# Two decode attentions on one core: the last group of heads ends in column form, with a new load order at the end

## The chip, the cores and the metric

The kernel runs on one core of a Trainium2 chip. The metric is device time in microseconds (us), the median of several executions. "Span" is the time from the first to the last instruction in the profile of one execution; it is 1.6 to 2.0 us less than the device time, except in three executions (2.9 to 3.4 us). Engines are called PE (matrix multiply), DVE (vector), ACT (scalar) and SP (here it only issues DMAs); POOL (general purpose) has no part in the ending. PE's granted clock, the share of full speed that PE was allowed, is recorded with each profile: in the records of the kernel before it is 1.00 or 0.50 and nothing else (another value in a table below is the mean of a stretch). A PE at full clock is called warm, one at half clock cold. "A's last p.v" is the last product of exponentials and V for problem A. All outputs are right.

Where a ratio of two kernels is given, it is the mean time of one kernel's runs over that of the other's in the same rounds, with a 95% interval. It is therefore not quite the ratio of the medians quoted beside it.

## The reference, cut to what matters

Problem A is decode attention of one token over 32 heads with 16384 keys each; problem B is the same over the last 4096 keys of its own cache. The head size is 128, and all data are bf16.

```python
q = (x @ wq) ...                       # one token, 32 heads of 128
scores = einsum("bhqd,bhkd->bhqk", q, k) * (128 ** -0.5)
p = softmax(scores)
o = einsum("bhqk,bhkd->bhqd", p, v)
out = o.reshape(1, 1, 32 * 128) @ wo   # 512 columns for A, 512 for B
```

K and V are read once: 336 MB of the 352 MB moved. The rest is weights.

## The kernel before

Work goes in units: four single heads of A (4 MB of K, 4 MB of V each), then one unit of B with four heads (also 4 + 4 MB), eight times over. A unit has two chunks of 64 keys per partition. For each chunk, DVE multiplies K by q (`prod`) and adds halves (`half`), PE sums further (`red`), DVE finishes the scores (`sc`), ACT takes the exponentials, and PE multiplies p by V (p.v).

```python
# one chunk
prod = kt * q                     # DVE 4.4 us
half = prod[:64] + prod[64:]      # DVE 2.3
red  = identity matmuls of half   # PE, 8 matmuls of 512 columns
sc   = reduce(red)                # DVE 0.7
p    = exp(sc)                    # ACT, once per head
acc += p.T @ vt                   # PE, 16 matmuls, p as weights, 512 columns
```

The loads stand in one queue on SP. A K or V load waits until one of two buffers is free. This is the end of the queue before the change (cut):

```python
cuts = {n - 1: (U, U), n: (U, U // 2, U // 2)}      # U = 64 keys
for i in range(n + 1):
    if i < n:
        ld.add("kt", lambda u=u: _load_kv(nc, cx, u, "k"))
        # ... wo, once in two groups, early
    if i:
        ld.add("vt", lambda u=units[i - 1], c=...: _load_kv(nc, cx, u, "v", c))
```

So the last loads are: K of A's head 31, V of head 30, K of B's last unit, V of head 31 in halves, V of B's last unit in a half and two quarters.

A group of four heads ends in row form. PE folds the accumulator into four rows, DVE and ACT divide, PE turns the rows into columns, and four matmuls with `wo` add to the output row:

```python
acc_sb = copy(acc)                 # ACT; for the last group half on DVE
f_ps   = fold(acc_sb)              # PE, sums of p in one column of it
orow   = f_ps * recip              # DVE, ACT
oc_ps  = columns of orow           # PE, 16 tiny matmuls
oc     = cast(oc_ps)               # DVE
out_ps += oc.T @ wo                # PE, 4 matmuls of 512 columns
row    = copy(out_ps); DMA         # ACT and DVE, after the last group
```

The softmax here doesn't subtract the row's maximum and nothing guards it: scores larger than these inputs give would overflow.

## Time and profile before

| what | value | where |
|---|---|---|
| device time | 836.6 us (835.41 to 836.83), 3 runs (the profiled one, at 835.15, is not among them) | result |
| span of the profiled run | 833.4 us | page |
| moved from HBM | 352.3 MB at 423 GB/s | page, part 3 |
| DVE, PE busy | 70%, 49% | page, part 1 |
| last K landed | 805.3 | DMA records |
| last V landed | 825.1 | DMA records |

This kernel has two levels of span. Of its 27 executions in the rounds of the experiments, 8 had a span of 833.3 to 833.8 us and 19 one of 834.8 to 836.1. The profile shows the shorter kind, and the longer has no trace. A ratio below mixes both levels, so it is not the ratio of two profiled spans.

The page's head and its slices (each digit is a fortieth of the span, in tenths of busy time):

```profile
span 833.4 us, 6067 instructions
DVE  2892666777777766777777766666677776677774
DMA  9999999999999999999999999999999999999994
```

DMA is busy at nine tenths or more until the last slice. What can move is the ending only. The chain of waits shows it; the columns are start, length and what, from the landing of the last K on (the rows left out are hand-overs of a few hundredths, and in the longer gaps more of the same kinds of work):

```profile
780.07 25.26 DMA kt<-in_B_k_cache_dram
...
817.74 2.21 DVE half L176
...
820.00 1.89 PE red L189 x8
821.88 1.00 PE acc_128 L236 x16
...
825.28 0.24 PE oc_ps L287 x15
825.52 0.97 PE acc_126 L236 x16
826.49 0.85 PE outA L306 x4
827.34 0.08 PE f_ps L260 x4
827.42 0.91 PE f_ps L265 x8
...
829.52 1.04 PE outB L306 x4
...
830.58 0.37 ACT rowB L318
...
830.98 0.41 DVE rowB L319
```

Read it as two bounds that meet. K lands at 805.33, and DVE works on it without a gap to 819.95 (its last `half` above ends there); its scores and exponentials are done at about 824.9. The last V lands at 825.07. The last p.v starts at 825.5, and from there to the end of the span takes 7.9 us. The two are 0.4 us apart: before that p.v PE was busy with A's columns (`oc_ps`), so in this execution it is K's chain that decides, with V close behind.

### The profile page before, as it was taken

What the parts mean: (1) busy time and instruction counts of PE and PEld (TensorE: products, weight loads), DVE (VectorE), ACT (ScalarE), POOL (GpSimd) and SP (SyncE); (2) the same over time, 40 slices, a digit from 0 to 9 for tenths busy, and PEclk for the clock granted to TensorE, in tenths of its full rate; (3) what the DMA queues carried; (4) which work ended last, traced back from release to release, by engine and by line L of the source; (5) the groups of instructions that cost most, each with busy time, mean ns of one, the idle gap of its engine ahead of it and who ended that gap; (6) DMA issues with size and microseconds to landing.
All of it is one profiled execution on the core that took longest, in us unless ns stands there. A gap on an engine that the chain in (4) does not pass through costs nothing.

```text
span 833.4 us, 6067 instructions
## 1 busy us (share of the span) xinstructions
PE 409.5 (49%) x2496; PEld 140.3 (17%) x2496; DVE 586.0 (70%) x301; ACT 68.8 (8%) x316; POOL 2.8 (0%) x16
## 2 busy tenths in 40 slices
PE   3356444544455445555455454465445444444446
PEld 1112111111121111211122111121112111111112
DVE  2892666777777766777777766666677776677774
ACT  2000011000110001000020000100011000110002
POOL 1000000000000000000000000000000000000000
PEclk9778667676777766776667765776667766777668
DMA  9999999999999999999999999999999999999994
GB/s 379 450 425 428 416 440 429 431 436 433 431 429 429 428 431 430 434 429 436 427 433 427 427 434 429 433 429 432 429 430 433 430 428 427 434 431 431 433 422 186
DMA packets 15599, 352.71 MB, mean 423 GB/s; under 512 B 2642, under 2 KB 2644, under 8 KB 4692
## 3 DMA queue, kind: packets, MB, share of 16 engines
q1 hardware_dynamic: 15284, 352.33, 98.6%
q8 instruction: 19, 0.31, 0.2%
q14 instruction: 8, 0.07, 0.0%
q10 hardware_dynamic: 288, 0.00, 0.0%
HBM read 352.32 MB, written 0.00 MB: 423 GB/s over the span
## 4 chain that ended last, share of the span: by engine, by line
DMA 67%; DVE 20%; issue 10%; PE 1%; SPq 1%; ACT 0%; DVEq 0%; ACTq 0%
DMA kt<-in_A_k_cache_dram 55%; DVE prod L164 12%; DMA kt<-in_B_k_cache_dram 12%; DVE half L176 6%; DVE sc L206 2%; SPq L156 1%; PE acc_126 L236 0%; PE red L189 0%; PE f_ps L265 0%; PE outB L306 0%; PE acc_128 L236 0%; PE outA L306 0%; DVE recip L275 0%; DVEq L164 0%; PE oc_ps L287 0%
## 5 line engine op out<-in xcount | busy, mean ns | idle before, releaser
L189 PE MATMUL red<-half,ident 128*128 128x512 bf16 x640 | 255.5, 572 | 390.0 <-DVE half L176 390.0
L164 DVE TENSOR_TENSOR prod<-kt,qallA 128x8192 bf16<-128x8192 bf16 x64 | 283.3, 4426 | 168.7 <-DMA kt<-in_A_k_cache_dram 168.0
L176 DVE TENSOR_TENSOR half<-prod 128x4096 bf16<-128x4096 bf16 x80 | 182.5, 2281 | 0.0
L189 PEld LDWEIGHTS <-ident 128*128 128x128 bf16 x640 | 82.9, 130 | 538.1 <-issue 512.5
L164 DVE TENSOR_TENSOR prod<-kt,qallB 128x8192 bf16<-128x8192 bf16 x16 | 70.8, 4426 | 51.9 <-DMA kt<-in_B_k_cache_dram 51.6
L206 DVE TENSOR_REDUCE sc<-red 128x64 f32<-128x512 f32 x80 | 54.7, 684 | 2.0 <-PE red L189 2.0
L213 ACT ACTIVATE p_sb<-sc,off 128x64 bf16<-128x64 f32 x64 | 21.5, 337 | 99.9 <-DVE sc L206 99.9
L236 PE MATMUL acc_126<-vt,p_sb 128*16 128x512 bf16 x256 | 20.3, 440 | 0.0
L265 PE MATMUL f_ps<-acc_sb,sel 128*4 128x128 f32 x128 | 16.6, 272 | 3.7 <-ACT acc_sb L251 3.7
L122 PE MATMUL q_ps<-wq_t,xbA 128*128 128x512 bf16 x32 | 8.4, 428 | 13.4 <-DMA wq_t<-in_A_wq_dram 13.4
L236 PE MATMUL acc_128<-vt,pA_122 128*16 128x512 bf16 x128 | 12.1, 518 | 5.3 <-DMA vt<-in_A_v_cache_dram 5.3
L236 PE MATMUL acc_128<-vt,pA_118 128*16 128x512 bf16 x128 | 11.1, 480 | 5.7 <-DMA vt<-in_A_v_cache_dram 5.7
L236 PE MATMUL acc_128<-vt,pA_110 128*16 128x512 bf16 x128 | 12.0, 514 | 0.0
L213 ACT ACTIVATION_READ_ACCUMULATOR p_sb<-sc,off 128x1 f32 x64 | 12.0, 187 | 0.0
L236 PE MATMUL acc_128<-vt,pA_114 128*16 128x512 bf16 x128 | 11.5, 494 | 0.0
L236 PE MATMUL acc_128<-vt,pA_120 128*16 128x512 bf16 x128 | 11.3, 489 | 0.0
L265 PEld LDWEIGHTS f_ps<-acc_sb,sel 128*4 128x4 f32 x128 | 9.9, 86 | 6.6 <-ACT acc_sb L251 4.5
L213 ACT ACTIVATE pA_124<-sc 128x64 bf16<-128x64 f32 x8 | 2.1, 256 | 106.6 <-DVE sc L206 106.6
L236 PE MATMUL acc_128<-vt,pA_116 128*16 128x512 bf16 x128 | 10.6, 462 | 0.0
L236 PE MATMUL acc_128<-vt,pA_112 128*16 128x512 bf16 x128 | 10.5, 460 | 0.0
L236 PE MATMUL acc_128<-vt,pA_124 128*16 128x512 bf16 x128 | 10.0, 442 | 0.0
L213 ACT ACTIVATE pA_116<-sc 128x64 bf16<-128x64 f32 x8 | 2.0, 256 | 90.6 <-DVE sc L206 90.6
(70 smaller groups left out, 142.9 us busy)
## 6 DMA issues: line engine op xcount, KB each, us to landing
kt<-in_A_k_cache_dram SPq DMA_DIRECT2D x32, 4096.0 KB, 27.1
vt<-in_A_v_cache_dram SPq DMA_DIRECT2D x31, 4096.0 KB, 31.0
kt<-in_B_k_cache_dram SPq DMA_DIRECT2D x32, 1024.0 KB, 24.0
vt<-in_B_v_cache_dram SPq DMA_DIRECT2D x28, 1024.0 KB, 28.3
wq_t<-in_A_wq_dram SPq DMA_DIRECT2D x1, 4096.0 KB, 12.5
wq_t<-in_B_wq_dram SPq DMA_DIRECT2D x1, 4096.0 KB, 23.7
wo_t<-in_A_wo_dram SPq DMA_DIRECT2D x4, 1024.0 KB, 29.2
wo_t<-in_B_wo_dram SPq DMA_DIRECT2D x4, 1024.0 KB, 29.7
```

Source lines behind the costliest of these rows:

```text
L122: cx.o(nc.tensor.matmul(q_ps[:, :], lhsT=st.xb[:, c, g, :], rhs=w[:, g, j * (512 // DH) : (j + 1) * (512 // DH), :], start=(g == 0 and c = ...
L156: cx.o(nc.sync.dma_start(out=t[g:P:n, k : k + w, :], in_=src[:, k : k + w, :]))
L164: cx.o(nc.vector.tensor_tensor(out=ch.prod[:, :, :], in0=u.kt[:, ch.k0 : ch.k0 + U, :], in1=q.rearrange("p (o d) -> p o d", o=1).broadcast ...
L176: cx.o(nc.vector.tensor_tensor(out=ch.half[:, :, :], in0=ch.prod[:, :, 0 : DH // 2], in1=ch.prod[:, :, DH // 2 : DH], op=ALU.add,))
L189: cx.o(nc.tensor.matmul(ch.red[:, :, :], lhsT=cx.ident[:, :], rhs=ch.half[:, :, b * W : (b + 1) * W], start=(b == 0), stop=(b == nb - 1),))
L206: cx.o(nc.vector.tensor_reduce(out=sc[:, :], in_=ch.red[:, :, :], axis=AX.X, op=ALU.add))
L213: cx.o(nc.scalar.activation(out=ch.p[:, :, g, :], in_=sc[:, :].rearrange("p (t e) -> p t e", e=4), func=ACT.Exp, scale=SCALE, bias=0.0 if ...
L236: cx.o(nc.tensor.matmul(gr.acc[r : r + 4 * G, :], lhsT=ch.p[:, t, :, :], rhs=u.vt[:, k : k + 4, :], start=(first and t < 4), stop=(last an ...
L265: cx.o(nc.tensor.matmul(gr.f_ps[:, 0:DH], lhsT=cx.sel[:, e, :], rhs=gr.acc_sb[e // 2][:, (e % 2) * DH : (e % 2 + 1) * DH], start=False, st ...
```

## The change

The intent is to shorten what stands behind the last byte. The last 32 keys of the last group use V as the weights, so that the result comes out as a column at once; the accumulator of the earlier keys is folded just before, so no fold or transposition stands behind the last byte. The output row is computed in quarters on four partitions, so that its copy is short. The last K goes between the halves of a V, and half of the last `wo` (0.5 MB) is loaded near the end, because it is needed late. Two copies that ran in halves, the second half on DVE (the last group's accumulator and A's output row), become one copy each, on ACT alone. Cut to the core:

```diff
+LATE = 32
-    cuts = {n - 1: (U, U), n: (U, U // 2, U // 2)}
+        if i == n - 2:
+            load_v(units[i - 1], 0, U)
+        elif i == n - 1:
+            load_v(units[i - 2], U, U)
+            load_v(units[i - 1])
+    load_v(u, 0, U)
+    load_v(u, U, U - LATE)
+    ld.add(None, lambda: _load_wo(nc, cx, stB, last_wo, 1))
+    load_v(u, 2 * U - LATE, LATE // 2)
+    load_v(u, 2 * U - LATE // 2, LATE // 2)
...
+def _late_fold(nc, cx, gr):            # accumulator as weights
+    for e in range(4):
+        matmul(gr.f_ps[:, 0, :], lhsT=gr.acc_sb[:, e * DH : (e + 1) * DH], rhs=cx.sel[:, e, :], ...)
+def _late_pv(nc, cx, ch, gr):          # V as weights
+    for k in range(U - LATE, U):
+        matmul(gr.f_ps[:, 0, :], lhsT=u.vt[:, ch.k0 + k, :], rhs=ch.p[:, k // 4, :, k % 4], ...)
+def _late_sum_before(nc, cx, st):      # partial output, in quarters
+    part = copy(st.out_ps[0:1, :])     # ACT
+    for t in range(4): matmul(st.out4[32 * t : 32 * t + 1, :], lhsT=ones_f[0:1, 0:1], rhs=part quarter t)
+def _late_out(nc, cx, gr):
+    oc = f_ps * recip                  # DVE
+    16 matmuls of 128 columns into out4; one ACT copy; DMA of 4 partitions
...
     _softmax(nc, cx, prev)
-    waiting.append(prev)
-    for ch in waiting: fin_pe(); fin_dve(); pv(ch)
-    while fins: fin_pe(); fin_dve()
+    fin_pe(); fin_dve()                # fold and row of A's last group
+    _late_sum_before(nc, cx, stB)
+    _late_sums(nc, cx, end)            # sums of p on all partitions
+    fin_pe(); fin_dve()                # columns of A
+    pv(waiting.pop(0))                 # B, chunk 0
+    fin_pe()                           # output of A
+    _pv(nc, cx, prev, 0, (U - LATE) // 4)
+    _late_fold(nc, cx, end)
+    _late_pv(nc, cx, prev, end)
+    _late_out(nc, cx, end)
```

## The prediction

> **What bounds the kernel now.** The page: 352.7 MB at 423 GB/s; DMA nine tenths busy in 39 of 40 slices; DVE 70%, PE 49%. The chain of waits is 67% DMA. No byte is saved, so only the tail can change. The last V piece lands 825.1 us into a span of 833.4 (trace): 8.3 us stand behind the last byte, and about 4 of them any ending needs (matmuls, a copy, the output DMA, 2.0 from issue to end).

> The timeline of the last 30 us shows a second bound. The last K (B, heads 28 to 31) lands at 805.3; DVE then runs 14.5 us without a gap to 820.0, the last reduction on PE ends 821.9, its scores 822.7, group A's last p.v 822.9; ACT copies A's accumulator (0.65) before the four exponentials (to 824.9). So K's chain and the last V end together at 825; the output row follows in 8.4 us.

> **What the change moves.** K passes 2 MB of V: 4.9 us earlier at the rate of the landings. Half a wo (0.5 MB, 1.2 us) goes to the end, so what stands before lands another 1.2 us earlier: last K at about 799.2, just when DVE is done with the unit before. DVE ends at 813.8 instead of 820.0. The last byte stays near 825.

> **What takes it back.** V of A's last head is no longer cut: it lands whole at about 813.9, and its first p.v stands before the last reduction in PE's order. That p.v (1.7 us at half clock) and the reduction (1.9 to 3.6) start on a cold PE, so A's last p.v ends at about 819.9 (819.0 to 821.3) instead of 822.9: 3 us gained of 6.

> From there the new order is longer. Estimates from the trace's durations, after that point: accumulator copy 0.75; exponentials to 2.1; row A on ACT to 2.5; ACT's copy of the partial output to 3.1, while PE waits; four fp32 matmuls and the sums to 4.0; transposition A, p.v of chunk 0, output A to 5.8; p.v of 32 keys to 6.4; ACT row A, then accumulator copy to 7.25; [...]oc 0.25; 16 output matmuls 0.5; row copy 0.3; DMA 2.0. About 13 us, against 10.5 before.

> [...]The trace has 96 ns for 128 bf16 columns, 85 for 4 or 16[...]; it has no fp32 load of 128 columns.

> So the span ends near 832.7, 0.7 less than before. PE and ACT, not the last landing, end it: when the last V lands I expect PE to be 2 us behind.

> **Predicted time** 835.7 us, 8 in 10 between 833.6 and 837.3. Faster by over 2%: 0.01; within 2%: 0.98; slower by over 2%: 0.01.

> **What would show it.** Last K landing 6 us earlier, no DVE wait before it; first p.v of A's last head ended by a V landing; PE waiting about 1.3 us for ACT's partial copy; the last p.v not waiting for V; output matmuls 0.5 instead of 1.0.

> **What would make it wrong.** PE warm at 814: 1 to 1.5 us faster. [...]Buffers freed later, so that the stream gets a gap: slower.[...]

Cuts in this text are marked. The sum came to about 13 us from A's last p.v to the end. Two of its terms are cut, the fold and the 32 p.v matmuls, because the trace before has no matmul of their kind (128 columns of weights, an operand of 4 columns); the terms that are left come to 10.3 us (7.25, then 0.25, 0.5, 0.3 and 2.0).

## The result, and the profile after

The changed kernel took 835.43 us (834.78 to 836.2, 4 runs) against 836.0 (835.34 to 836.83, 4 runs): ratio 0.9993, interval 0.9976 to 1.0010. No difference is shown. Two profiles, 832.8 and 833.4 us of span, say the same.

Here are the page's lines that answer to those of before:

```profile
span 832.8 us, 6118 instructions
DVE  2892666777777766777777766666677776777791
DMA  9999999999999999999999999999999999999995
```

DVE's last busy slices moved forward: its last two digits are 91 instead of 74. The stream did not get shorter (the last V landed at 825.09 against 825.07). This is the chain of waits after the change, down to the output copy; the output DMA is issued at 830.04:

```profile
782.63 31.16 DMA vt<-in_A_v_cache_dram
...
813.84 1.89 PE acc L248 x16
815.72 3.24 PE red L202 x8
818.97 1.00 PE acc L248 x16
...
820.04 0.58 ACT acc_sb L259
820.63 1.33 ACT p_sb L226 x8
821.96 0.34 ACT orow L360
822.30 0.48 ACT late_part L302
...
822.82 0.39 PE out L307 x8
823.22 0.54 PE f_ps L267 x4
823.76 0.23 PE oc_ps L370 x15
823.98 0.97 PE acc L248 x16
824.95 0.42 PE outA L389 x2
...
825.84 0.47 ACT rowA L400
...
826.36 0.59 ACT acc_sb L259
...
826.99 1.05 PE f_ps L278 x8
828.05 0.82 PE f_ps L290 x32
...
829.11 0.62 PE out L325 x16
...
829.75 0.27 ACT late_row L332
```

The chain no longer starts at the last K. It starts at V of A's last head, and it passes by the last V, which landed at 825.09: the matmuls that need its keys start at 828.31 (the last 16 of the 32 in the line `f_ps L290`). From A's last p.v (ended 819.9) on, PE and ACT take turns with hardly a gap.

This table sets the landmarks side by side. Times are from the DMA and instruction records of each profiled execution, in us from the start of the span.

| | before | after |
|---|---|---|
| last K landed | 805.33 | 799.17 |
| DVE's last `half` ended | 819.94 | 813.77 |
| A's last p.v ended | 822.85 | 819.94 |
| last V landed | 825.07 | 825.09 |
| output DMA issued | 831.41 | 830.04 |
| end of span | 833.41 | 832.79 |
| from A's last p.v to the end | 10.55 | 12.85 |
| from the last V to the end | 8.34 | 7.70 |

K came 6.2 us earlier. A's last p.v came only 2.9 earlier, and the rest of the ending grew by 2.3.

### The profile page after: what moved, and what is told of

Its sections match the earlier page's. It is cut to its first block, busy times and chain, and to the rows that moved or that the text cites. A ratio compares the mean times of both kernels' runs of the same rounds, so it can differ in the third digit from the quotient of the medians.

```text
span 832.8 us, 6118 instructions
## 1 busy us (share of the span) xinstructions
PE 410.6 (49%) x2524; PEld 141.4 (17%) x2524; DVE 585.0 (70%) x299; ACT 68.3 (8%) x301; POOL 2.9 (0%) x16
## 4 chain that ended last, share of the span: by engine, by line
DMA 68%; DVE 19%; issue 10%; PE 2%; SPq 1%; ACT 0%; DVEq 0%; ACTq 0%
DMA kt<-in_A_k_cache_dram 55%; DVE prod L177 12%; DMA kt<-in_B_k_cache_dram 9%; DVE half L189 6%; DMA vt<-in_A_v_cache_dram 4%; DVE sc L219 2%; PE red L202 1%; SPq L170 1%; PE acc L248 1%; ACT p_sb L226 0%; ACT acc_sb L259 0%; PE f_ps L278 0%; PE outA L389 0%; PE f_ps L290 0%; PE out L325 0%
## 5 line engine op out<-in xcount | busy, mean ns | idle before, releaser
L248 PE MATMUL acc<-vt,pA 128*16 128x512 bf16 x1024 | 87.7, 476 | 17.2 <-DMA vt<-in_A_v_cache_dram 17.1
L226 ACT ACTIVATE pA<-sc 128x64 bf16<-128x64 f32 x64 | 16.4, 256 | 520.8 <-DVE sc L219 520.8
L248 PEld LDWEIGHTS <-pA 128*16 128x16 bf16 x1024 | 23.3, 98 | 87.0 <-issue 79.5
L248 PE MATMUL acc<-vt,p_sb 128*16 128x512 bf16 x248 | 21.4, 467 | 0.0
L259 ACT COPY acc_sb<-acc 128x512 f32<-128x512 f32 x16 | 9.4, 585 | 85.6 <-PE acc L248 85.6
L226 ACT ACTIVATION_READ_ACCUMULATOR pA<-sc 128x1 f32 x64 | 11.9, 186 | 0.0
L248 PEld LDWEIGHTS <-p_sb 128*16 128x16 bf16 x248 | 5.6, 99 | 17.1 <-issue 15.6
L389 PE MATMUL outA<-wo_t,oc 128*1 128x512 bf16 x32 | 8.2, 379 | 0.0
L124 PE MATMUL q_ps<-wq_t,xbB 128*128 128x512 bf16 x32 | 7.2, 378 | 1.7 <-DMA wq_t<-in_B_wq_dram 1.1
L389 PE MATMUL outB<-wo_t,oc 128*1 128x512 bf16 x28 | 7.7, 402 | 0.0
```

The source lines that it names most:

```text
L124: cx.o(nc.tensor.matmul(q_ps[:, :], lhsT=st.xb[:, c, g, :], rhs=w[:, g, j * (512 // DH) : (j + 1) * (512 // DH), :], start=(g == 0 and c = ...
L226: cx.o(nc.scalar.activation(out=ch.p[:, :, g, :], in_=sc[:, :].rearrange("p (t e) -> p t e", e=4), func=ACT.Exp, scale=SCALE, bias=0.0 if ...
L248: cx.o(nc.tensor.matmul(gr.acc[r : r + 4 * G, :], lhsT=ch.p[:, t, :, :], rhs=u.vt[:, k : k + 4, :], start=(first and t < 4), stop=(ends an ...
L259: cx.o(nc.scalar.copy(gr.acc_sb[:, :], gr.acc[:, :]))
L389: cx.o(nc.tensor.matmul(st.out_ps[0:1, :], lhsT=gr.oc[:, j : j + 1], rhs=st.wo_t[i][:, g, j * st.DN : (j + 1) * st.DN], start=(gr.i == 0 a ...
```

## The experiments

Ten runs. Each kernel is compared with the kernel before in the same rounds. In the diffs `-` is the changed kernel unless said otherwise.

### The new load order alone

This is the kernel before with the loads of the changed one:

```diff
-    cuts = {n - 1: (U, U), n: (U, U // 2, U // 2)}
+    # K between the V halves, half of wo (in rows) near the end, V pieces as in the changed kernel
+    # ending: row form, as before
```

> The kernel before with the new load order alone (K between the V halves, half of wo near the end, the new cuts of the last V), row-form ending kept. Theory (two bounds met at 825: K's chain and the last V landing; the order frees K's chain only): last landing stays at 825.1, A's last p.v ends about 819.9, only the last four p.v matmuls stand behind the last landing, and the row ending takes 7 us from there: span about 832.1, so as good as or better than the full change (832.8). Rival (the column form is what pays): span 833.4 as before, the full change is better by 0.6.

The run gave 836.02 us, ratio 0.9987 (0.9972 to 1.0002), span 832.7. The last V landed at 825.20 and A's last p.v ended at 819.56. The span was 0.6 longer than the theory's number, because A's output still stands behind the last landing on PE:

```profile
822.69 2.51 DMA vt<-in_B_v_cache_dram
...
825.24 0.39 PE acc L243 x4
825.63 0.85 PE outA L313 x4
826.49 0.08 PE f_ps L267 x4
826.56 0.91 PE f_ps L272 x8
```

The chain now hangs on the last V. The load order alone reaches what the whole change reaches (832.7 against 832.8). The column ending, as ordered, added nothing to it. The three executions without a trace were longer, with spans of 834.3 to 834.4, against 833.2 to 834.3 for those of the changed kernel in its first rounds; both kernels have a ratio to before whose interval holds 1.

### The column ending alone

This is the changed kernel with the loads of before:

```diff
-        if i == n - 2:
-            load_v(units[i - 1], 0, U)
-        elif i == n - 1:
-            load_v(units[i - 2], U, U)
-            load_v(units[i - 1])
+        if i == n - 1:
+            load_v(units[i - 1], 0, U)
+            load_v(units[i - 1], U, U)
+    # wo whole and early; the last V in 64 + 32 + 32 keys
```

> The changed kernel with the old load order (K behind V, wo early, A's last V in halves, the last V cut at 64 and 96), column-form ending kept. Theory (the column ending as ordered is a 12.9 us chain on PE and ACT from A's last p.v on, 2.4 longer than the row ending): A's last p.v at 822.9, span about 835.8, so slower than before by 2.4. Rival (the column form is shorter behind the last landing and gains by itself): span below 833.4.

It took 839.5 us, ratio 1.0035 (1.0020 to 1.0050): slower than before by 2.9 us (0.0035 of 836.8), where 2.4 was expected. A's last p.v ended at 823.24, as before the change, and 14.34 us followed. The expected 12.9 is missed by 1.4; the PE clock accounts for 0.8 of it in the fold alone. The fold, eight fp32 loads of 128 columns, each with a matmul of 4 columns, took 1.05 us in the changed kernel (131 ns a pair) at a clock of 1.00, and here 1.87 (234 ns a pair), the first of these lines:

```profile
831.17 1.87 PE f_ps L278 x8
833.04 0.87 PE f_ps L290 x32
```

The clock granted to PE was 1.00 from 825.1 to 828.5 and 0.50 from 828.5 to 832.0, where the table of stretches ends. By itself the new ending is a loss; the load order hides it.

### V of A's last head in two loads

```diff
-            load_v(units[i - 1])
+            load_v(units[i - 1], 0, U)
+            load_v(units[i - 1], U, U)
```

> The changed kernel, but V of A's last head in two loads again. Theory (the first p.v of that head waits for the whole V until 813.8 and then stands 1.8 us before the last reduction on PE): that p.v runs near 809.5, the reduction starts at 813.9, A's last p.v ends about 818.2 instead of 819.9, and as everything behind it is one chain the span falls by the same 1.7 to about 831.1. Rival (the last landing at 825.1 sets the end): A's last p.v moves, the span stays at 832.8.

It took 834.96 us, ratio 0.9976 (0.9957 to 0.9994). The profiled execution had a span of 833.6; the four executions ran from 830.2 to 833.9. The first p.v did leave the place ahead of the reduction, which started at 813.93 instead of 815.65. But A's last p.v ended at 819.32, only 0.6 earlier:

```profile
813.93 3.57 PE red L202 x8
817.51 1.84 PE acc L248 x15
```

Both ran at half clock: the stretch table has 0.50 from 812.8 to 819.6, after a stretch in which PE was busy for 1.46 of 3.40 us. Of the 1.7 us by which the reduction starts earlier, 0.3 goes into the reduction (3.57 us against 3.24 in the changed kernel, where the clock was full again at 818.5) and 0.8 into the p.v behind it (1.84 against 1.00). My number was wrong for that reason in this execution. The span is longer than the changed kernel's 832.8 because the clock fell to half once more, from 823.1 to 826.5 us (0.51 in the table), so 14.33 us followed A's last p.v instead of 12.85. One execution of the four had a span of 830.2; it has no trace, so its cause is not shown, and its device time of 833.62 is 3.4 us above its span, so it was only 0.9 below the next one.

### The output in one row

```diff
-    _late_sum_before(nc, cx, stB)
 def _late_out(nc, cx, gr):
-    for j in range(G):
-        for t in range(4): matmul(st.out4[32 * t : 32 * t + 1, :], ...)   # 128 columns
-    row = copy(st.out4); DMA of 4 partitions, 256 bytes each
+    for j in range(G):
+        matmul(st.out_ps[0:1, :], ...)                                    # 512 columns
+    row = copy(st.out_ps[0:1, :]); DMA of one partition, 1024 bytes
```

> The changed kernel with column-form p.v, but the output in one row of the running accumulator: no copy of the partial output and no four fp32 matmuls; 4 output matmuls of 512 columns instead of 16 of 128, one row copy of 512, one DMA row. Theory (the quarters cost more than they give): minus 0.9 for the partial copy and its matmuls on the ACT and PE chain, plus 0.4 matmuls, plus 0.3 copy, minus 0.8 for the DMA, whose issue to end of span is 2.75 us with 4 rows against 1.97 with one: span about 831.9. Rival (the quarters pay): span 833.5.

It took 834.51 us, ratio 0.9974 (0.9959 to 0.9988), with all four executions between 834.35 and 834.64. From A's last p.v to the end took 12.24 us against 12.85: minus 0.6, where 0.9 was expected. This one profile started its ending 0.7 later (A's last p.v at 820.65), so its span of 832.9 is not shorter. The DMA gave 0.55 of it, where 0.8 was expected: 2.19 us from issue to the end of the span against 2.74. The issue itself is seen on SP's timeline (start, length), here in one row and then, in the changed kernel, in four:

```profile
830.70 0.26 SPq L330 DMA_DIRECT2D out_dram<-late_row  x1
```

```profile
830.04 0.61 SPq L333 DMA_DIRECT2D out_dram<-late_row  x1
```

The quarters cost more than they give: without them the partial copy and its matmuls (0.85 in all) and 0.55 of the DMA go, and the output matmuls (1.04 against 0.62) and the copy (0.57 against 0.27) come to 0.72 more.

### The changed kernel again, as a control

> The changed kernel as it is, again, as the control of the other three runs of this call (same chip, same rounds). Both theories: 835.4 give or take 0.7, ratio to before between 0.998 and 1.0005; from A's last p.v to the end 12.9 us if the PE clock stays full there, up to 1.5 more where a window at half clock falls into it.

It took 835.85 us, ratio 0.9991 (0.9978 to 1.0004). The spans were 833.3, 833.4, 834.1, 834.6 and 834.7, which is about two levels. The profiled one is 834.1. It was ahead until A's last p.v (819.29), and then took 14.78 us instead of 12.85. The table of stretches tells the two executions apart (columns: stretch, its length, busy time and count of PE, weight loads, DVE, ACT and POOL, granted PE clock, DMA share, GB/s). First this run, then the first profile of the changed kernel:

```profile
821.00:824.40 3.40, 2.29 (x50) 1.36 (x50) 0.67 (x4) 1.12 (x4) 0.00 (x0) 1.00 0.72 243
824.40:827.80 3.40, 2.64 (x14) 0.84 (x13) 0.00 (x0) 1.16 (x2) 0.00 (x0) 0.50 0.03 11
827.80:831.20 3.40, 2.93 (x55) 2.55 (x55) 0.16 (x1) 0.17 (x1) 0.00 (x0) 0.50 0.00 0
```

```profile
821.90:825.40 3.50, 2.58 (x53) 1.50 (x54) 0.52 (x4) 0.87 (x3) 0.00 (x0) 1.00 0.49 162
825.40:828.80 3.40, 2.65 (x47) 1.95 (x42) 0.00 (x0) 1.10 (x2) 0.00 (x0) 1.00 0.00 0
```

The same instructions ran at full clock to 828.8 in one execution, and at half clock from 824.4 in the other. In the clock records of the two profiles of before and after, all but the last of each last 3.41 us or a whole multiple of it (to 17.07), and the changes fall at other places in each execution: at 818.2 and 831.8 in the kernel before, at 818.5 and 828.8 in the changed one, at 824.4 in the control. The ending leaves PE with pauses (1.10 us for the partial copy, 0.76 for the accumulator copy, in both executions of the changed kernel), so I take it to depend on where these steps fall; that is a guess, which two executions fit and do not prove.

### A's output later

```diff
-    fin_pe()                           # output of A
     _pv(nc, cx, prev, 0, (U - LATE) // 4)
+    fin_pe()
     _late_fold(nc, cx, end)
```

> The changed kernel, but A's four output matmuls and its row copy come after the p.v of B's 32 keys and their accumulator copy. Theory (from A's last p.v on the ending is one serial chain through PE and ACT, so what is moved out of it comes off the end): B's accumulator copy starts about 0.75 earlier, A's output fills PE while it waits for that copy, span minus 0.7, about 832.1. Rival (PE is not on the chain at that point, the accumulator copy waits for something else): no change of the time from A's last p.v to the end (12.9).

It took 834.62 us, ratio 0.9980 (0.9968 to 0.9992). Its fold took 1.80 us, near the control's 1.87 at half clock and far from the 1.05 at full clock, so I take its clock to have been at half there too, and compare the two: 14.08 us from A's last p.v to the end against 14.78, which is the 0.7 expected. The span (833.6) must not be held against the 832.8 of an execution with the better clock.

### Keeping PE's clock up

```diff
         _red(nc, cx, ch)
+        if c == len(chunks) - 2:
+            for _ in range(16):        # results never read
+                matmul(idle[:, :], lhsT=cx.ident[:, :], rhs=ch.half[:, 0:8, :], ...)
```

> The changed kernel with 16 matmuls of no use (512 columns, into a spare bank) in PE's wait before A's last V, so that the PE clock is granted in full when that V lands. Theory (the half clock between 811.7 and 818.5 costs the first p.v of that head and the last reduction 2.3 us): p.v 1.0 instead of 1.9, reduction 1.9 instead of 3.3, A's last p.v ends about 817.7, span about 830.7 if the clock stays full. If the dummies themselves run at half clock they end after the landing and cost up to 2 us; then the theory is not tested by that execution. Rival (the clock is of no weight, the chain is set by DVE and ACT): the p.v is shorter, the span stays 832.8.

It took 833.17 us, ratio 0.9967 (0.9952 to 0.9983), again spread: spans of 830.5, 830.6, 830.8, 832.1 and twice 834.2. Three of six hit the theory's 830.7, but none of the three has a trace, so it is not shown that their clock stayed full. The profiled one is one of the two longest: its p.v took 1.0 and its reduction 1.8 at a clock of 1.00 (811.1 to 821.3), so A's last p.v ended at 818.03, 1.9 earlier than in the first profile of the changed kernel. Then the clock fell to 0.50 at 821.3 and 16.19 us followed. The half clock at the start of the chain is a true cost (1.9 us here), and the clock later in the chain is another.

### The version that the reasons suggest

```diff
+    pv(waiting.pop(0))                 # B, chunk 0, straight after A's last p.v
     fin_pe(); fin_dve()                # fold and row of A
-    _late_sum_before(nc, cx, stB)
-    _late_sums(nc, cx, end)
+    _pv(nc, cx, prev, 0, (U - LATE) // 4)
     fin_pe()                           # columns of A
+    _late_sums(nc, cx, end)
     fin_dve()
-    pv(waiting.pop(0))
     fin_pe()                           # output of A, while ACT copies
-    _pv(nc, cx, prev, 0, (U - LATE) // 4)
     _late_fold(nc, cx, end)
 # with the output in one row, and A's last V in two loads
```

> The version that the theory suggests: A's last V in two loads, output in one row, and the ending reordered: p.v of B's chunk 0 straight after A's last p.v, p.v of 32 keys as soon as the exponentials are there, then A's transposition and output while ACT copies. Theory: the PE and ACT chain now ends before the last landing, so the last V decides: 16 matmuls 0.45, oc 0.4, output 1.05, row copy 0.6, DMA 2.2 behind the landing at 825.2: span about 829.9, time from the last V landing to the end 4.7 against 7.7, ratio to before about 0.996. Rival (something else than this chain holds the end): span above 831.5.

It took 832.68 us (832.1 to 833.24, 5 runs) against 836.8: ratio 0.9953 (0.9941 to 0.9965), with a span of 830.4 in the profile. From the last V to the end took 4.83 us, where 4.7 was expected. The last V landed at 825.57 in this run, 0.4 later than the 825.2 reckoned with, and the second 16 matmuls start behind it: they paused for 0.15 us.

```profile
824.41 0.98 PE f_ps L278 x8
825.40 0.40 PE f_ps L290 x16
...
825.81 0.56 PE f_ps L290 x16
...
826.61 1.04 PE outB L322 x4
...
827.67 0.57 ACT late_row L329
```

### The same order with the row ending

This is the run with the load order alone, plus A's last V in two loads, and A's whole ending ahead of the last p.v (`-` is that run):

```diff
-    waiting.append(prev)
-    for ch in waiting: fin_pe(); fin_dve(); pv(ch)
+    pv(waiting.pop(0))
+    fin_pe(); fin_dve(); fin_pe(); fin_dve(); fin_pe()
+    pv(prev)
```

> The row-form ending of before with everything else as in the best version: new load order, A's last V in two loads, p.v of chunk 0 straight after A's last p.v, all of A's ending ahead of the last p.v. Theory (once nothing but the last landing decides, the column form shortens what stands behind it): behind the landing stand four p.v matmuls 0.4, accumulator copies 0.8, half a fold 0.5, reciprocal, row, transposition, cast 1.2, output 1.0, two row copies 0.8, DMA 2.2: 7.0 from the last V landing to the end against 4.8 in the best version, span about 832.2, ratio to before about 0.998. Rival (the form of the ending is of no weight, only order is): 4.8 to 5.3, span about 830.4.

It took 834.51 us, ratio 0.9987 (0.9973 to 1.0001), span 832.5, and 7.29 us from the last V to the end (7.0 expected). Here the last landing decides:

```profile
822.74 2.51 DMA vt<-in_B_v_cache_dram
...
825.34 0.42 PE acc L243 x4
```

So the column form is worth 2.5 us (7.29 less 4.83) once A's work is out of the way. The device times of the same rounds say the same: 834.51 here against 832.03 for the column form in the next run. About 0.2 of that is the row copy in two parts (0.37 + 0.41 here, 0.57 in one).

### The suggested version without the cut

It is the version above with A's last V in one load.

> The best version without its cut of A's last V. Theory: A's last p.v ends about 0.5 to 1.2 later than in the best version (819.5 to 820 against 818.7), as the whole V lands at 814; the ending has about 1 us to spare before the last landing, so the span rises by 0 to 0.7, to 830.4 to 831.1, ratio to before 0.996. Rival (the cut is what made the best version fast, the order and the row do little): span 832 or more.

It took 832.03 us (831.82 to 832.26, 5 runs) against 835.48: ratio 0.9953 (0.9941 to 0.9966), span 830.3. A's last p.v ended at 819.66, one microsecond later than with the cut, and the end did not move. From A's last p.v to the end took 10.69 us: the ending is 2.2 shorter than the changed kernel's, 0.6 of which the single row gave in its own run above. The cut of V is worth nothing here. In this profile the 32 matmuls run without a pause, from 825.30 on, and the last 16 start 0.5 us after the last V landed (825.20): PE's chain still ends a little later than the landing. From there to the end it took 5.15 us. So the two bounds nearly meet again; by this profile a shorter chain alone could give no more than about 0.5 us.

## Why the prediction was right or wrong

The time was right (835.7 predicted, 835.43 measured), and so were the two steps that it rests on.

- **Two bounds met at 825: right.** With K early and the row ending kept, the chain hangs on the last V (first experiment). With K late and the column ending, it is the 2.9 us slower that the longer ending costs (second).
- **K 6 us earlier, 3 us of it kept: right.** K landed at 799.17 (799.2 predicted), DVE ended at 813.77 (813.8), A's last p.v at 819.94 (819.9). DVE waited 0.15 us for K.
- **The new ending is longer, 13 us against 10.5: right as a sum** (12.85 against 10.55), with errors inside it that cancel, so that the sum fits so well is in part luck. The output DMA took 2.74, not 2.0; 0.55 of that is its four rows (2.19 with one row). The output matmuls took 0.62, not 0.5. The fold took 1.05 and the 32 p.v matmuls 0.82, together less than the two cut terms gave them. PE waited 1.1 us for the partial copy (1.3 predicted). The clock had fallen to half at 828.8, before the output matmuls.
- **PE behind when the last V lands: right.** The fold starts 1.9 us after the landing (826.99 less 825.09), where the prediction's own sum puts it (819.9 + 7.25, 2.05 after). The matmuls that need the last V stand behind the fold and the first 16, and start 3.2 us after it.
- **Weight loads.** Weight load and matmul together took 26 ns a pair in the changed kernel (32 pairs of 128 bf16 columns with a matmul of 4 columns in 0.82 us; 0.87 at a clock of 0.50, in the control), and the landing did not decide. Taking even these 0.82 us out of a chain that is 3 us behind does not bring it level.
- **"PE warm at 814: 1 to 1.5 us faster": too small.** With the clock at 1.00 from 811.1 to 821.3 A's last p.v came 1.9 us earlier, and three of six executions ended near 830.6, 2.2 less than the changed kernel's best execution (832.8), though without a trace.
- **Missed:** the clock after 820. I took it as full. It falls to half within the ending in some executions and costs 1.9 us there (14.78 against 12.85).
- **V's missing cut** was named among what takes the gain back. That the p.v waits for the whole V is shown by the chain. That the cut would give much back is not: A's last p.v gained 0.6 with it in the changed kernel and 1.0 in the reordered one, where the end did not move.

So the expected gain went into two places: a waiting p.v and a reduction that began at half clock (3 of 6 us; the clock was 0.50 from 811.7 to 818.5), and a longer serial ending (2.3 us) that ACT and PE walk in turns. The column form is good only after the serial parts are moved ahead of the last landing; then it is worth 2.5 us.

It stays open what sets PE's granted clock. The upper level of the kernel before, to which most of its executions belong, is not explained either. Each run has one trace, so a part of a microsecond read from two profiles rests on one execution of each.

## What to carry to other kernels

At the end of a stream-bound kernel, find the last landing, then list what stands behind it and what still runs from before. Shortening the work that needs the last byte pays only when everything else is out of its way, so reorder first and reform second. When a small ending differs from run to run, look at the granted clock there before explaining the difference.
